# A gated linear recurrence with a feed-forward block behind it: q and k transposed by DMA from slab 8, f16 sums and an SBUF carry from the second block, one product for q and k, a new order

## The chip, the cores and the metric

The kernel runs on one core of a Trainium2 chip. A core has five engines, each with an instruction queue of its own that is worked off in order: TensorE (PE, matmuls; its weight loads are listed as PEld), VectorE (DVE), ScalarE (ACT), GpSimd (POOL) and SyncE (SP, which here issues nearly all DMA transfers). They wait for one another on semaphores. Matmul results land in PSUM, which has 8 banks of 128 x 512 f32; everything else lies in SBUF, 128 partitions wide. Transfers run on 16 DMA engines.

The metric is the device time of one execution in microseconds, median over runs.

## The reference

Sizes: batch B = 4, heads H = 8, sequence S = 768, head width D = 48, feed-forward width 1536.

```
scale = min(|a|, 0.999) / (|a| + 1e-6);   a_n = a * scale        # a = a_re + i a_im, per position and channel
for t in range(S):
    S_re, S_im = a_re_n*S_re - a_im_n*S_im + k[t] v[t]^T,  a_re_n*S_im + a_im_n*S_re
    y[t] = q[t] . S_re
x   = y as [B*S, H*D] = [3072, 384]
out = (sigmoid(x @ w_gate) * (x @ w_val)) @ w_out
```

So a linear attention whose state decays and turns by a complex factor per step, then a gated feed-forward block. The output is f32, [3072, 384].

## The kernel before, in words

**Slabs.** The sequence is cut into 6 blocks of 128 steps; a slab is one block of one batch element, 24 in all, numbered block by block (slab m is block m // 4, batch element m % 4). Slabs are handled in 8 groups (`SIZES` = 2, 2, 4, 4, 4, 4, 2, 2); groups 0 and 1 are block 0, group 2 is block 1, groups 6 and 7 are block 5.

**Running sums in place of the recurrence.** Within a block the product of the factors up to step t is exp(sum of log magnitudes) times a turn by the sum of the angles. Per slab:

- `lr`, `la` load a_re and a_im; `sq`, `add` form the squared magnitude; `lna`, `lnm`, `inv` (Ln, Ln, Exp on ACT), `lh` (the cap), `r` and `atan` (the angle), the ACT steps once per group.
- `cl` (L664, L668): a matmul with a triangular matrix gives the running sum of log magnitudes. Groups in `SPLIT` use two f16 matmuls, a high part (`lh`) and a low part (`ll`, on DVE, L637); the others use one f32 matmul, which the trace records as two instructions. `ee` takes exp of it with both signs.
- `ct` (L794): the same for the angles. Split groups first form a high part `th` and a low part `tl` (L779, DVE). `r16` and `nid` (L809, L816) take the whole turns off.
- **The carry.** The angle at the end of a block must be added in the next. `cr` (L826) copies the last rows of the sum of slab b into rows 32b to 32b+31 of a tile. For block 1 (`0 < c <= PECARRY`) a matmul with `sel_t` (L799) adds it in PSUM. For blocks 2 to 5 `car` (L749, on SP) writes the four rows of that tile to DRAM, and `hop` (L756, on POOL, an accumulating transfer) adds them to the first row of the angles, behind `atan` and ahead of `th`.
- `ab`, `cs` (Abs and two Sin on ACT, in PSUM) give cosine and sine. `ks` and `qs` (L862, both DVE) multiply k and q (scaled by `qke`) with them into a slot of two tiles; six slots go round.
- For the scores q and k must lie with channels on partitions. Slabs below 12: `tp` (L905, L906), 16 TensorE transposes into PSUM in two halves, and `qkT` (L912, DVE) copies each half to SBUF. Slabs in `CROSSED` (12 to 23): `xk` and `xq` (L883), transposing DMA transfers issued on SP.
- `sc` (L924) the scores, `mst` (L939) the causal mask, `kv` and `P` (L971, L981) the state update, `u` and `x16` the decayed state for the next block, `y` (L997, L999) the output, `y16`, `xp`, `xt` bring it, transposed, to the feed-forward block.

**Feed-forward.** Pairs of slabs (`PAIR` = 2) go through six rounds of `pg`, `pv` (L1056, 6 matmuls of 256 columns each), `tanh` (L1067, ACT) and `p` (L1074, DVE), then `po` (L1095), `ot` and the store `st`. Three `xt` and three `p` tiles allow three pairs in flight.

**What sets the order.** Every step has a due time in the table `TIMES`. The function `order` sorts all steps by due time; each engine gets its instructions in that order and never passes a waiting one. `SLOTS` says which buffer (which PSUM bank, for `ps`) each step takes, in the order of first use. `HOME` gives, for steps that several engines can do, one letter per slab (per pair for `lh`, `r`, `th`): v DVE, a ACT, g POOL. `WARM` puts matmuls of zeros ahead of some steps. ACT's function tables are reloaded (L1138) where the order asks for another set.

Of the kernel before, what the change touches and what calls it, by code (L numbers as in the profile page):

```python
# [27 lines left out]
CROSSED = range(12, 24)  # L28
YCROSSED = ()
PAIR = 2  # L30
PECARRY = 1
SPLIT = range(3, 8)
MSTP = ()
HOME = {
    "sq": "vavvgaagaggagagavaaggggg",
    "add": "gggvggvvgggggggggggggggg",
    "lh": "vggggggggggg",
    "r": "vvggvgggvggg",
    "v16": "gggaggagggggggaaagggvggv",
    "qke": "vvvggggggggggggggggggggg",  # L40
    "th": "aaaavvaaggvv",
    "ab": "vvaaaaaaavaaaavaaaaaavaa",
    "u": "gggggggggggggggvgggg",
    "x16": "ggggggggggvgggag",
    "y16": "vvaaaaaaavavvaaaaavavaaa",
    "xt": "vvaavvavvvvavavvavvvaaaa",
    "ot": "vaaavvavaavavaaaaaavavava",
# [4 lines left out]
        34.76, 27.25, 44.96],  # L52
    "wv": [
        36.69, 44.14, 47.99],
    "wo": [
        63.7, 71.27, 80.15],
    "lr": [
        0.75, 1.65, 12.17, 12.18, 15.95, 26.45, 24.02, 15.96, 37.53, 42.64,
        54.85, 37.54, 58.8, 63.25, 87.47, 78.78, 95.08, 110.69, 105.75,
        114.39, 170.85, 174.29, 130.56, 139.74],  # L60
    "la": [
        1.12, 4.55, 12.22, 12.2, 19.37, 25.84, 21.22, 16.03, 42.84, 42.83,
        53.55, 44.17, 80.31, 59.39, 76.31, 78.76, 107.5, 95.09, 117.2, 119.03,
        170.87, 174.28, 139.73, 134.75],
    "sq": [
        4.54, 6.39, 12.23, 12.21, 21.17, 27.26, 24.93, 19.27, 49.71, 42.85,
        55.51, 53.38, 81.42, 80.11, 88.29, 90.2, 115.95, 126.32, 117.31,
        127.19, 176.25, 177.54, 155.55, 165.32],
    "add": [
        6.4, 7.31, 12.44, 12.45, 23.07, 30.13, 25.79, 24.29, 52.32, 54.49,  # L70
        56.06, 56.07, 83.14, 87.29, 98.5, 94.17, 119.01, 127.85, 126.29,
        128.49, 176.26, 179.52, 155.57, 165.52],
    "lna": [
        7.32, 12.83, 30.15, 57.36, 94.15, 129.61, 180.39, 165.33],
    "lh": [
        10.88, 13.61, 30.14, 26.43, 64.31, 64.98, 101.75, 107.3, 134.76,
        140.3, 182.76, 169.83],
    "lnm": [
        12.47, 15.44, 31.38, 58.76, 101.74, 130.55, 181, 165.54],
    "inv": [  # L80
        7.9, 13.59, 31.37, 66.41, 94.18, 135.41, 180.4, 165.34],
    "r": [
        8.79, 15.45, 34.73, 34.72, 70.42, 69.22, 96.98, 101.73, 138.82, 139.7,
        180.42, 179.54],
    "cl": [
        15.49, 15.46, 19.34, 21.21, 36.7, 34.06, 31.47, 38.64, 74.99, 66.39,
        67.33, 68.54, 104.43, 105.41, 108.6, 112.42, 145.37, 136.86, 146.77,
        143.53, 184.79, 185.77, 172.31, 172.64],
    "ee": [
        15.9, 15.48, 24.01, 25.83, 38.98, 38.19, 37.4, 40.76, 75.51, 67.18,  # L90
        67.86, 69.16, 106.4, 106.51, 110.29, 112.99, 146.78, 137.85, 147.62,
        144.73, 186.41, 187.2, 174.3, 173.16],
    "scr": [
        25.85, 33.29, 31.51, 31.5, 52.27, 52.93, 51.21, 47.17, 78.8, 78.75,
        79.05, 78.79, 117.22, 114.38, 121.64, 120.31, 154.92, 148.93, 150.85,
        148.91, 193.01, 193.02, 185.81, 187.21],
    "rbt": [
        33.49, 34.96, 54.47, 80.32, 126.28, 155.54, 195.56, 198.13],
    "arr": [
        34.71, 36.72, 56.03, 81.16, 126.73, 155.99, 197.32, 199.92],  # L100
    "lk": [
        12.19, 12.46, 21.28, 29.68, 26.44, 48.23, 42.63, 55.5, 64.32, 78.77,
        68.33, 64.97, 110.67, 96.74, 95.11, 108.94, 102.79, 145.39, 138.23,
        145.62, 147.68, 165.3, 187.24, 187.22],
    "lq": [
        12.24, 13.6, 21.95, 31.49, 31.48, 51.2, 42.67, 58.78, 66.4, 83.19,
        69.2, 92.61, 112.7, 96.75, 106.52, 118.39, 105.76, 154.09, 154.91,
        147.66, 185.12, 168.96, 202.83, 187.26],
    "lv": [
        13.62, 27.35, 15.47, 33.78, 59.27, 59.25, 72.81, 65.62, 92.62, 76.82,  # L110
        98.51, 94.16, 118.36, 112.69, 118.02, 147.65, 161.33, 145.61, 165.55,
        133.7, 178, 187.25, 145.6, 208.24],
    "v16": [
        15.43, 32.35, 37.52, 36.75, 60.61, 61.26, 73.19, 66.75, 95.1, 76.83,
        110.26, 114.74, 119.98, 126.08, 125.91, 150.87, 165.56, 145.71,
        171.38, 137.86, 201.11, 188.09, 202.82, 213.05],
    "qke": [
        19.36, 16.02, 24.92, 34.87, 41.51, 52.28, 47.18, 58.79, 81.41, 84.14,
        80.33, 98.48, 118.19, 110.61, 126.3, 119.99, 148.92, 156, 158.45,
        168.57, 196.68, 192.98, 206.64, 191.8],  # L120
    "atan": [
        9.99, 19.31, 36.74, 71.94, 103.78, 140.31, 183.16, 184.81],
    "ct": [
        10.87, 12.16, 21.18, 27.27, 37.41, 45.83, 41.33, 51.19, 78.06, 81.17,
        84.17, 88.31, 112.74, 114.95, 122.26, 124.27, 147.09, 152.92, 163.2,
        166.33, 189.04, 188.71, 201.82, 200.42],
    "r16": [
        19.28, 15.91, 21.19, 28.21, 39.67, 48.9, 44.18, 52.45, 78.74, 81.4,
        84.19, 91.31, 113.27, 116.35, 122.79, 125.25, 147.61, 154.08, 165.57,
        167.78, 191.29, 189.24, 202.38, 201.83],  # L130
    "nid": [
        19.29, 15.94, 21.2, 30.12, 40.75, 50.35, 44.79, 53.37, 80.1, 84.16,
        84.23, 95.06, 114.37, 117.19, 123.9, 125.89, 148.28, 154.72, 166.17,
        168.59, 192.14, 190.02, 205.29, 204.07],
    "cr": [
        19.33, 21.23, 21.27, 34.74, 41.1, 52.3, 47.13, 53.95, 83.15, 87.38,
        86.81, 95.66, 114.73, 119.02, 127.22, 128.51, 150.86, 157.12, 167.36,
        168.95],
    "ab": [
        19.32, 19.3, 21.96, 32.37, 41.09, 52.29, 47.14, 54.84, 83.2, 86.85,  # L140
        86.82, 96.76, 117.32, 119.18, 124.29, 128.5, 152.28, 157.11, 166.97,
        169.87, 195.82, 190.82, 206.62, 205.63],
    "cs": [
        19.35, 21.24, 21.97, 34.75, 42.73, 52.33, 47.15, 56.04, 84.18, 88.32,
        86.84, 96.77, 118, 119.97, 127.23, 128.52, 152.3, 157.13, 167.76,
        170.15, 196.48, 191.79, 208.25, 205.64],
    "ks": [
        21.25, 21.94, 27.34, 37.42, 45.18, 52.92, 48.24, 59.38, 84.21, 88.36,
        87.36, 98.49, 120.32, 122.63, 127.84, 129.14, 153.43, 157.77, 169.85,
        174.96, 196.69, 193, 210.87, 206.28],  # L150
    "qs": [
        21.26, 23.09, 28.68, 37.59, 45.19, 55.52, 48.25, 60.62, 86.8, 89.74,
        88.3, 99.12, 121.63, 123.92, 128.54, 129.58, 153.44, 158.42, 170.16,
        174.97, 196.7, 193.63, 210.88, 206.65],
    "tp": [
        23.08, 25.81, 27.29, 25.8, 32.34, 29.67, 39.45, 40.77, 47.12, 47.77,
        56.59, 56.15, 51.18, 62.13, 63.23, 66.72, 88.44, 87.35, 92.59, 95.63,
        93.04, 94.14, 106.39, 100.14],
    "qkT": [
        23.68, 31.36, 30.17, 27.28, 33.16, 33.77, 40.14, 44.16, 50.38, 50.39,  # L160
        58.81, 59.26, 52.31, 64.33, 72.69, 69.17, 89.14, 88.34, 94.19, 96.97,
        99.53, 95.05, 107.82, 104.77],
    "sc": [
        27.79, 32.12, 31.15, 27.56, 37.93, 38.47, 41.08, 44.95, 53.53, 53.15,
        58.82, 61.25, 68.32, 68.87, 73.45, 71.92, 91.07, 90.84, 94.59, 98.88,
        108.15, 96.73, 111.48, 108.37, 126.06, 129.13, 132.19, 130.66, 142,
        139.81, 148.44, 148.67, 163.53, 160.38, 165.06, 165.29, 178.02,
        176.24, 180.57, 181.01, 202.37, 202.15, 198.9, 198.67, 216.75, 216.53,
        213.04, 212.16],
    "mst": [  # L170
        30.16, 32.56, 32.36, 31.16, 38.46, 39.07, 41.5, 47.19, 54.48, 54.56,
        59.29, 62.16, 69.19, 75.52, 76.84, 76.32, 95.04, 91.95, 95.64, 100.13,
        110.24, 97.62, 112.43, 109.59, 131.96, 132.01, 132.72, 132.21, 142.42,
        140.29, 150.22, 150.21, 165.07, 161.65, 166.19, 166.34, 179.53,
        180.41, 180.99, 182.09, 203.42, 202.81, 199.32, 200.04, 217.64,
        216.95, 215.36, 215.97],
    "kv": [
        25.82, 33.79, 40.87, 39.9, 64.09, 65.61, 75.31, 71.06, 100.86, 97.61,
        116.99, 124.06, 152.07, 143.86, 147.63, 167.81, 180.36, 169.82,
        177.12, 180.16],  # L180
    "P": [
        27.3, 34.95, 42.66, 40.74, 66.74, 66.42, 78.07, 73.71, 101.76, 101.07,
        120.33, 125.9, 156.46, 146.79, 150.2, 168.56, 183.82, 170.94, 177.52,
        185.8],
    "y": [
        33.28, 34.7, 42.62, 47.57, 65.81, 63.68, 75.54, 79.69, 98.47, 101.72,
# [200 lines left out]
def kernel(  # L387
# [12 lines left out]
    nc = tc.nc  # L400
# [134 lines left out]
    def add(key, emit, **kw):  # L535
        plan.add(key, emit, **kw)
        return key
# [637 lines left out]
```

## Time and profile before

| what | us |
|---|---|
| median of 11 runs | 251.26 (249.84 to 255.63) |
| the profiled execution | 250.66 |
| its span, first to last instruction | 248.9 |

| engine | busy us | share | instructions |
|---|---|---|---|
| PE | 222.6 | 89% | 2318 |
| DVE | 205.8 | 83% | 341 |
| ACT | 201.7 | 81% | 330 |
| POOL | 151.9 | 61% | 152 |

The DMA engines moved 38.63 MB, mostly in packets of 192 bytes (48 f32, one head of one step).

Busy time of PE is from the start of a matmul to its modelled end, and matmuls overlap: how fast PE really gets on is read from one start to the next. A row of the groups reads: line, engine, operation, out<-in by name, shapes, count, then busy us and mean ns of one, then the engine's idle time just before them and what ended it. A row of the waits reads: who waited for whom, total us, times, longest.

### The profile page before, as it was taken

The numbers are of one execution on the slowest core, as the hardware profiler recorded it, in microseconds if no ns is written. First come the engines' busy times: TensorE is split into PE (matmuls) and PEld (weight loads), VectorE is DVE, ScalarE is ACT, GpSimd is POOL, SyncE is SP. The second block draws the span as 40 slices with busy tenths as digits, with TensorE's granted clock in tenths as the row PEclk, the third lists the DMA queues.
The fourth block names the chain that finished last, engine by engine and source line by source line (L and its number), as shares of the span: only waits on it lengthen the run. The fifth ranks groups of instructions, "written<-read, shape, count | busy, mean of one in ns | idle before, by whom it ended". The sixth has DMA issues, their size and how long they took to land.

```text
span 248.9 us, 6100 instructions
## 1 busy us (share of the span) xinstructions
PE 222.6 (89%) x2318; PEld 172.8 (69%) x2318; DVE 205.8 (83%) x341; ACT 201.7 (81%) x330; POOL 151.9 (61%) x152
## 2 busy tenths in 40 slices
PE   0175899999989789999999999899999999999994
PEld 0132666678868457888767788677778877787883
DVE  6569998989889698999999979679986989878341
ACT  2999999979879589999989999787999992562441
POOL 5237596857998596777488663979567774500000
PEclk9999589999999999999999999999999999999999
DMA  7999899998999934687849998838798518563111
GB/s 141 213 207 205 162 191 209 195 210 169 189 173 188 192 79 88 124 179 175 171 89 212 202 201 154 205 90 177 165 209 178 106 67 175 122 126 76 65 66 63
DMA packets 158333, 38.63 MB, mean 155 GB/s; under 512 B 151248, under 2 KB 158304, under 8 KB 158304
## 3 DMA queue, kind: packets, MB, share of 16 engines
q1 hardware_dynamic: 154160, 34.68, 67.5%
q0 software_dynamic: 4144, 3.56, 9.5%
q8 instruction: 18, 0.29, 0.5%
q14 instruction: 11, 0.09, 0.1%
HBM read 30.70 MB, written 4.74 MB: 142 GB/s over the span
## 4 chain that ended last, share of the span: by engine, by line
PE 43%; ACT 7%; POOL 4%; DMA 2%; issue 2%; DVE 1%; SPq 1%; POOLq 0%
PE banks L1056 21%; PE banks L1095 14%; DMA v<-in_v_dram 2%; PE banks L924 2%; ACT L1138 2%; POOL a L653 1%; PE banks L794 1%; PE banks L1031 1%; ACT g L1067 1%; PE banks L999 1%; PE banks L668 1%; PE banks L997 1%; POOL qk L734 1%; PE banks L971 1%; POOL lh L628 1%
## 5 line engine op out<-in xcount | busy, mean ns | idle before, releaser
L1074 DVE SCALAR_TENSOR_TENSOR p<-g,banks 128x512 f16<-128x512 f16 x72 | 48.2, 682 | 13.3 <-ACT g L1067 6.8
L1067 ACT ACTIVATE g<-banks 128x512 f16<-128x512 f32 x72 | 41.6, 604 | 21.3 <-PE banks L1056 16.2
L1056 PE MATMUL banks<-xt,wv 128*128 128x256 f16 x432 | 57.1, 272 | 0.0
L1056 PE MATMUL banks<-xt,wg 128*128 128x256 f16 x432 | 56.4, 272 | 0.1
L1095 PE MATMUL banks<-wo,p 128*128 128x384 f16 (+1 forms) x300 | 55.0, 319 | 0.3 <-DVE p L1074 0.2
L1056 PEld LDWEIGHTS <-wg 128*128 128x128 f16 x432 | 41.0, 98 | 7.0 <-issue 1.3
L734 POOL TENSOR_TENSOR qk<-qk,ee 128x768 f32<-128x768 f32 x21 | 40.6, 1938 | 8.1 <-ACT ee L678 3.4
L1056 PEld LDWEIGHTS <-wv 128*128 128x128 f16 x432 | 40.7, 98 | 6.4 <-issue 0.2
L1138 ACT ACT_TABLE_LOAD x30 | 38.5, 1283 | 0.5
L1095 PEld LDWEIGHTS <-p 128*128 128x128 f16 x300 | 27.6, 98 | 13.2 <-issue 0.4
L939 DVE TENSOR_TENSOR mst<-banks,msk_t 128x512 f16<-128x512 f32 x48 | 31.9, 685 | 2.1 <-PE banks L924 1.6
L597 POOL TENSOR_TENSOR lm<-sq 128x384 f32<-128x384 f32 x21 | 21.9, 1050 | 12.1 <-DVE sq L591 7.8
L591 POOL TENSOR_TENSOR sq<-a 128x768 f32<-128x768 f32 x11 | 17.1, 1555 | 14.1 <-DMA a<-in_a_im_dram 10.7
L862 DVE TENSOR_TENSOR kst<-qk,banks 128x768 f16<-128x768 f32 x24 | 22.8, 949 | 1.9 <-issue 0.9
L862 DVE TENSOR_TENSOR qst<-qk,banks 128x768 f16<-128x768 f32 x24 | 22.7, 947 | 0.0
L794 PE MATMUL banks<-a,wt_t 128*128 128x384 f32 x16 | 8.9, 658 | 12.1 <-ACT a L741 11.3
L653 POOL TENSOR_TENSOR a<-a 128x768 f32<-128x768 f32 x8 | 14.5, 1814 | 4.4 <-ACT a L647 4.3
L912 DVE COPY qkT<-banks 128x1024 f16<-128x1024 f16 x24 | 16.2, 684 | 0.7 <-PE banks L906 0.7
L905 PE MATMUL banks<-idn_t,kst 128*128 128x128 f16 x96 | 14.1, 229 | 2.2 <-DVE state L981 1.1
L924 PEld LDWEIGHTS <-qkT 128*128 128x128 f16 x192 | 13.9, 100 | 2.6 <-issue 0.6
L906 PE MATMUL banks<-idn_t,qst 128*128 128x128 f16 x96 | 14.1, 230 | 0.6 <-DVE qst L862 0.6
L809 DVE TENSOR_SCALAR r<-banks 128x384 f16<-128x384 f32 x24 | 13.2, 551 | 1.3 <-PE banks L794 1.0
(95 smaller groups left out, 433.8 us busy)
## 6 DMA issues: line engine op xcount, KB each, us to landing
a<-in_a_re_dram SPq DMA_DIRECT2D x24, 192.0 KB
a<-in_a_im_dram SPq DMA_DIRECT2D x24, 192.0 KB
qk<-in_k_dram SPq DMA_DIRECT2D x24, 192.0 KB
qk<-in_q_dram SPq DMA_DIRECT2D x24, 192.0 KB
v<-in_v_dram SPq DMA_DIRECT2D x24, 192.0 KB
out_dram<-ot SPq DMA_DIRECT2D x23, 192.0 KB
wg<-in_moe_w_gate_dram POOLq DMA_DIRECT2D x3, 384.0 KB, 5.2
wv<-in_moe_w_val_dram POOLq DMA_DIRECT2D x3, 384.0 KB, 6.5
```

What stands on the lines that cost most here:

```text
L591: on.tensor_tensor(out=T[SQ], in0=T[A][:, :, s], in1=T[A][:, :, s], op=ALU.mult)
L597: home("add", m).tensor_tensor(out=T[LM][:, s], in0=T[SQ][:, 0], in1=T[SQ][:, 1], op=ALU.add)
L653: home("r", w).tensor_tensor(out=T[A][:, 1, i:j], in0=T[A][:, 1, i:j], in1=T[A][:, 0, i:j], op=ALU.mult)
L734: home("qke", m).tensor_tensor(out=T[QK], in0=T[QK], in1=T[EE], op=ALU.mult)
L862: nc.vector.tensor_tensor(out=T[SL][i].rearrange("p h (r x) -> p h r x", r=2)[:, :, :, 0:D], in0=heads(T[QK][:, i]).unsqueeze(2) .broadcas ...
L924: nc.tensor.matmul(sc[:, 4 * hf * both + i], kt, qt, start=True, stop=True)
L939: nc.vector.tensor_tensor(out=T[MS][:, :n_], in0=T[SC], in1=msk_t.unsqueeze(1).broadcast_to([L, n_, L]), op=ALU.mult)
L1056: nc.tensor.matmul(T[ACC][:, r], wt[:, j, f0:f0 + 128], T[XT][:, :, j], start=(j == 0), stop=(j == 2))
L1067: nc.scalar.activation(out=T[G16], in_=T[PG], func=FT.Tanh, scale=0.5)
L1074: nc.vector.scalar_tensor_tensor(out=T[PT][:, 2 * fp:2 * fp + 2], in0=T[G16], scalar=1.0, op0=ALU.add, in1=T[PV], op1=ALU.mult)
L1095: nc.tensor.matmul(T[PO][:, :wd], T[PT][:, fb, s0:s0 + L], wo16[:, fb, c0:c0 + wd], start=(fb == 0), stop=(fb == NFB - 1))
L1138: nc.scalar.preload_act_table_set(SETS[key[1]])
```

## The change

Five edits and new tables.

1. `CROSSED` starts at slab 8: slabs 8 to 11 are transposed by DMA too; 16 halves are left for TensorE in place of 24.
2. `PECARRY` 0: block 1 gets its carry by a `hop` as well, and `sel_t` and its matmul go. All hops (six in place of five) read the SBUF tile of `cr` directly; `car` and its DRAM tiles go. A hop waits for `atan` of its group and for `cr` of its own slabs.
3. `SPLIT` starts at group 2: the sums of slabs 4 to 7 are f16 pairs.
4. `ks` and `qs` become one product of 128 x 1536 elements (`qs`); the two tiles of a slot become one. `kv`, `tp`, `xk` and `xq` wait for it.
5. `qkT` and `P` get a letter in `HOME`; `qkT` is on DVE throughout, `P` of slab 0 on ACT.

`HOME`, `TIMES`, `SLOTS` and `WARM` are new throughout. In the new order slabs 22 and 23 come to their end before 20 and 21. The tables `TIMES` and `SLOTS` are left out here.

```diff
-CROSSED = range(12, 24)
+CROSSED = range(8, 24)
-PECARRY = 1
-SPLIT = range(3, 8)
+PECARRY = 0
+SPLIT = range(2, 8)
 HOME = {
-    "sq": "vavvgaagaggagagavaaggggg",
-    "add": "gggvggvvgggggggggggggggg",
-    "lh": "vggggggggggg",
-    "r": "vvggvgggvggg",
-    "v16": "gggaggagggggggaaagggvggv",
-    "qke": "vvvggggggggggggggggggggg",
-    "th": "aaaavvaaggvv",
-    "ab": "vvaaaaaaavaaaavaaaaaavaa",
-    "u": "gggggggggggggggvgggg",
-    "x16": "ggggggggggvgggag",
-    "y16": "vvaaaaaaavavvaaaaavavaaa",
-    "xt": "vvaavvavvvvavavvavvvaaaa",
-    "ot": "vaaavvavaavavaaaaaavavava",
+    "sq": "aavvgaaaaaaaaaggaaagaaag",
+    "add": "gvvvgggggggggvvggggvvgvg",
+    "lh": "ggvgggggggvg",
+    "r": "gggvvggggvgv",
+    "v16": "gggvgaggvvggggaggvggggvg",
+    "qke": "vvgggggggvggggggggggggvg",
+    "th": "aavggggagaag",
+    "ab": "vvavvaaavvvvaavvvaaaaaav",
+    "qkT": "vvvvvvvvvvvvvvvvvvvvvvvvvvvvvvvvvvvvvvvvvvvvvvvv",
+    "P": "avvv",
+    "u": "ggggggggggggvggvgggv",
+    "x16": "gggvggaggggvvaga",
+    "y16": "vvavaaaaavvaavaavvavaaaa",
+    "xt": "vvvvvvvavvvvvvavvvvvaaaa",
+    "ot": "vvvavvvvvvvavvavvaaavavaa",
 }
 WARM = {
-    ('ct', 2): 6,
-    ('sc', 1, 0): 5,
-    ('cl', 6): 1,
-    ('cl', 5): 2,
-    ('sc', 2, 0): 7,
-    ('cl', 7): 1,
-    ('pg', 1, 0): 1,
-    ('pv', 1, 0): 2,
-    ('pg', 1, 5): 1,
+    ('cl', 0): 10,
+    ('sc', 0, 0): 11,
+    ('sc', 1, 1): 1,
+    ('y', 0): 12,
+    ('sc', 2, 1): 1,
+    ('kv', 0): 2,
+    ('sc', 3, 0): 12,
+    ('pv', 0, 0): 3,
+    ('y', 2): 4,
+    ('pv', 0, 3): 2,
+    ('sc', 5, 1): 6,
 }
...
-        qs = const.tile([L, H, L], F16, name=f"qst{i}")
-        ks = const.tile([L, H, L], F16, name=f"kst{i}")
...
+        t = const.tile([L, 2, H, L], F16, name=f"slot{i}")
...
         if c > PECARRY:
-            if not lo:
-                def e(T, CRP=cr_tile[c - 1], c=c):
-                    nc.sync.dma_start(car[c - 1], T[CRP][31::32])
-
-                car_key = add(("car", g), e,
-                              after=[cr_key[m0 + s - B] for s in range(B)],
-                              use=[cr_tile[c - 1]])
-
-            def e(T, A=A, c=c, lo=lo, n=n):
+            def e(T, A=A, CRP=cr_tile[c - 1], lo=lo, n=n):
                 nc.gpsimd.dma_start(
-                    T[A][:1, 1, :n], car[c - 1][lo:lo + n].unsqueeze(0),
+                    T[A][:1, 1, :n],
+                    T[CRP][32 * lo + 31:32 * (lo + n):32],
                     accum_op=ALU.add)
 
-            key = add(("hop", g), e, after=[("atan", g), car_key], use=[A])
+            key = add(("hop", g), e,
+                      after=[("atan", g)] + [cr_key[m0 + s - B] for s in range(n)],
+                      use=[A, cr_tile[c - 1]])
...
-            for i, nm in ((1, "ks"), (0, "qs")):
-                def e(T, SL=SL, i=i, QK=f"qk_{m}", CS=CS):
-                    nc.vector.tensor_tensor(
-                        out=T[SL][i].rearrange(
-                            "p h (r x) -> p h r x", r=2)[:, :, :, 0:D],
-                        in0=heads(T[QK][:, i]).unsqueeze(2)
-                        .broadcast_to([L, H, 2, D]),
-                        in1=T[CS][:, :, :HD].rearrange("p r (h d) -> p h r d", d=D),
-                        op=ALU.mult)
...
+            def e(T, SL=SL, QK=f"qk_{m}", CS=CS):
+                nc.vector.tensor_tensor(
+                    out=T[SL].rearrange("p i h (r x) -> p r i h x",
+                                        r=2)[:, :, :, :, 0:D],
+                    in0=T[QK].rearrange("p i (h d) -> p i h d", d=D)
+                    .unsqueeze(1).broadcast_to([L, 2, 2, H, D]),
+                    in1=T[CS][:, :, :HD].rearrange("p r (h d) -> p r h d", d=D)
+                    .unsqueeze(2).broadcast_to([L, 2, 2, H, D]),
+                    op=ALU.mult)
+
+            add(("qs", m), e, after=[("cs", m), ("qke", m)], new=[SL],
+                use=[f"qk_{m}", CS])
...
-                add(("kv", m), e, after=[("ks", m), ("v16", m)], new=[KV],
+                add(("kv", m), e, after=[("qs", m), ("v16", m)], new=[KV],
                     use=[SL, V16])
```

## The prediction

> **What bounds the kernel now.** I read the stretches of the span first, then the PE timeline, then the groups of instructions and the waits. Stretches: start:end and length, then busy us of PE, PEld, DVE, ACT and POOL, the granted clock, the DMA share and GB/s.
>
> ```profile
> 10.90:33.00 22.10, 16.05 (x92) 10.15 (x92) 19.60 (x28) 21.69 (x33) 12.19 (x12) 0.85 1.02 193
> 33.00:100.00 67.00, 62.62 (x691) 48.23 (x689) 60.50 (x99) 59.15 (x100) 53.59 (x51) 1.00 0.94 171
> 100.00:140.00 40.00, 39.25 (x434) 31.34 (x433) 38.50 (x62) 38.18 (x61) 30.01 (x30) 1.00 0.77 159
> 140.00:200.00 60.00, 58.90 (x667) 47.50 (x666) 50.53 (x84) 55.09 (x92) 40.45 (x37) 1.00 0.80 166
> 200.00:231.00 31.00, 31.00 (x317) 23.75 (x316) 25.47 (x41) 15.89 (x33) 10.89 (x9) 1.00 0.52 113
> 231.00:248.90 17.90, 14.73 (x131) 11.85 (x127) 5.60 (x9) 6.04 (x12) 0.00 (x0) 1.00 0.19 67
> ```
>
> From 33 us on PE is busy 191.8 of 198 us up to 231. A busy matmul is not a matmul at full rate, so I also added up the usual distance from one start to the next, shape by shape (56 ns for a 128-column transpose, 109 for 256 columns, 162 for 384): 209.9 us of the 234.2 between the first start and the last. Of the 24 left over, 12.6 lie before 40 us, half clock (25.8 to 32.6 us) included, and 11 behind. So after the head **PE sets the pace, but DVE and ACT are close behind**: in 100 to 140 us DVE is busy 38.50 of 40 (96.3%) and ACT 38.18. Before 33 us PE is not the limit: ACT is busy 21.7 of 22.1 us, DVE 19.6, and the DMA share is 1.02. From 231 us on only the feed-forward part is left, with DVE at a third.
>
> **The change, TensorE.** The price of a step is read from starts (start, us, instruction):
>
> ```profile
> 36.98 0.91 PE L664 MATMUL banks<-lm,wl_t 128*128 128x384 f32 x2
> 37.73 0.33 PE L1031 MATMUL banks<-idn_t,y 128*128 128x128 f16 x3
> 37.90 0.86 PE L794 MATMUL banks<-a,wt_t 128*128 128x384 f32 x2
> 38.69 0.91 PE L799 MATMUL banks<-cr,sel_t 32*128 32x384 f32 x2
> 39.53 0.56 PE L1144 MATMUL banks<-zero 128*128 128x128 f16 x7
> ```
>
> and from the chain of work (start, time to the next piece), where the f16 form stands:
>
> ```profile
> 146.45 0.33 PE banks L668 x2
> ```
>
> An f32 sum `cl` holds PE from 36.98 to 37.73, 0.75 us; as two f16 matmuls it holds 0.33. Four slabs (4 to 7): 4 x 0.42 = 1.7 us less. The f32 sum `ct` holds 37.90 to 38.69, 0.79, against 0.33: 4 x 0.46 = 1.8. The carry product with `sel_t`, 38.69 to 39.53, goes: 4 x 0.84 = 3.4. The transposes of slabs 8 to 11 go: 4 x 16 x 0.056 = 3.6. Together **10.5 us** of PE, all of it work done after 33 us. Added are 64 warming matmuls in place of 26, 38 x 0.056 = 2.1 us. They precede steps of the head, where PE idles about 6 of 22 us; I take 0, bounds 0 and 2.1.
>
> **The change, DVE.**
>
> ```profile
> L1074 DVE SCALAR_TENSOR_TENSOR p<-g,banks 128x512 f16<-128x512 f16 x72 | 48.2, 682 | 13.3 <-ACT g L1067 6.8
> L862 DVE TENSOR_TENSOR kst<-qk,banks 128x768 f16<-128x768 f32 x24 | 22.8, 949 | 1.9 <-issue 0.9
> L912 DVE COPY qkT<-banks 128x1024 f16<-128x1024 f16 x24 | 16.2, 684 | 0.7 <-PE banks L906 0.7
> L597 DVE TENSOR_TENSOR lm<-sq 128x384 f32<-128x384 f32 x3 | 1.6, 550 | 0.0
> ```
>
> Off DVE: 8 copies `qkT` x 0.684 = 5.5. The two products of a slab, 949 ns each, start 0.87 apart and hold DVE 1.82 us. One of 1536 columns isn't in the trace; 384 columns more cost 0.948 - 0.548 (state update, 128x384) = 0.40, so 0.948 + 0.80 = 1.75. Gain 24 x 0.07 = 1.7; bounds 0 (the two already overlap all that can be saved) and 3.5 (a whole fixed part goes, 0.948 - 0.80 = 0.15). I take 1.7, from the nearest rows. On DVE: group 2 becomes split, with two `ll` of 1.00 and two `tl` of 1.22 us: 4.4. Counting the letters of the home table at the rows' own durations: `ab` 5 to 12 (7 x 0.56 = 3.9), `ot` 9 to 16 (3.7), `add` 3 to 8 (2.75), `xt` 14 to 18 (1.4), `v16` 2 to 5 (1.5), `u`, `x16`, `y16` two more each (2.9), `lh` and `qke` one more each (1.9); `sq` two fewer, `th` three fewer, `P` one fewer (-4.1). That is +14.1. Sum: 14.1 + 4.4 - 5.5 - 1.7 = 11.3; since instructions back to back start some 0.08 us before the last one's recorded end and 28 more come, it can be as low as 9. I take **+10 us on DVE**.
>
> **The others.** ACT gives up `ab`, `ot`, `xt`, `v16`, `y16` (11.2 us), takes eight `sq` (8 x 0.846 = 6.8), `x16`, `th` and a `P` (2.4), and by the new order reloads its table 29 times for 30 (1.28): -3.3. POOL gives up 21 us (`sq`, `add` above all) and takes 4. DMA: eight transposing transfers; those in the trace are 1024 packets of 256 B at 21.3 ns, 1.36 us of all 16 engines each, so +10.9 us. They come where the DMA share is 0.77 and nothing waits; I take 0, and if that cover is gone 10.9. SP issues them in 1.28 us each, 10.3 us, less four `car` issues of 0.56. Behind a waiting transpose on SP stand loads of `a`, `q`, `k`, `v` and stores:
>
> ```profile
> SPq L883 <- DVE qst L862: 12.3, 6, 5.7
> SPq L883 <- PE banks L1056: 8.1, 8, 1.3
> SPq L749 <- ACT banks L838: 3.4, 1, 3.4
> ```
>
> (waits of SP's queue: total us, times, longest). All its waits for L883 come to 35 us, 1.5 per transpose, so 12 us more, in a stretch (90 to 130 us) where it issues 24 of 40 us; loads run slabs ahead, so 0. Scores of a crossed slab start 4.8 us after its q product ends (130.6 to 135.4), by TensorE about 2.6; PE has feed-forward products (11.8 us per pair of slabs: 12 x 0.654 + 6 x 0.652) to put there. A rule speaks against this part: the Trainium skill, "VectorE: DVE Perf Modes", section "The three transpose paths", gives 390 ns for a 128x128 transpose on TensorE and 1309 ns on the crossbar, and advises TensorE where PSUM will do. By it 64 blocks would be an estimated 84 us of transfers, and the kernel would get slower; the trace, with eight blocks in 1.28 us of issue and 1.36 us of transfer, does not agree.
>
> **The carry.** Four hops now read SBUF, not the DRAM copy written by `car`. Nothing waits for `car` today: it is issued at 67.7, 104.5, 141.7 and 188.0 us, the hop 7 to 10 us behind, held by the arctangent (POOL's `hop` waited 5.9 us for ACT). So the shorter way is worth 0, plus SP's 3.4 us wait. But block 1 gets a hop that it did not have:
>
> ```profile
> L756 POOL DMA_DIRECT2D a<-car x5: 803/838/882, 77.7 to 202.0; - x5
> DMA to landing us min/median/max: 2.2/2.7/5.6
> ```
>
> It holds POOL, and what is queued there (`qke`, `lh`), for 0.84 us, and lands 2.2 to 5.6 us after its issue (5.6 is the one at 77 us, under a full DMA as here), then `th` 0.83 and `tl` 1.22 before `ct` of slabs 4 to 7. In the trace that `ct` follows its arctangent by 0.3 us (36.12 + 1.49 to 37.90); it will come 4.3 to 7.7 later. The cover is two pairs of feed-forward products, 23.6 us. I take 0; without cover 7.7. "DMA: Bandwidth & Descriptors" in the skill, section "Anatomy of one DMA", puts a transfer of this queue at about 2.0 us; by it the delay would be near the lower end, and the 5.6 us in the trace shows more.
>
> The order ends with slabs 20 and 21 in place of 22 and 23, so the last store is a whole slab, not the half that slab 23 has: about +0.3 us (`ot` 0.48 for 0.33, and twice the bytes). `kv` waits for the joint product, 0.87 us more; PE has other work. The rest of the new order I can't price: its bound is what PE stalls now, 11 us behind the head and about 6 in it, in either direction; I take 0.
>
> **The sum.** PE alone gives -10.5. DVE does not let all of it through. Between 4 and 231 us it is busy 197.4 of 227 us, 87%. With 10 more, 207.4, nothing is gained at a share of 91.4%; at 96.3%, the best that it holds over 40 us, the stretch takes 215.4 and the PE gain comes whole. I take the middle, 93.8%: 207.4/0.938 = 221.1, a gain of 5.9. The profiled execution, 250.66 us (span 248.9 and 1.8 around it), would become 244.8. The median of the runs shown, 251.26, lies 0.6 above, so **245.4 us**.
>
> **Rivals.** (1) **PE alone bounds**: DVE's waits, 13.3 us before `p` above all, are waits for PE and ACT and shrink with them. Then 251.26 - 10.5 = 240.8. For it: PE's share; against it: DVE's 96% with no wait to spare at 100 to 140. (2) **The gain is used up at the start**: the new hop, under a DMA share of 0.94 to 1.02, is not covered because the second pair's `xt` is late as well. 7.7 + 2.1 (warming) + 0.3 against 10.5 leaves 250.9. Against it: twelve products of pair 0 can be run any time. (3) **DVE becomes the bound**, the slower side: one queue in order, with more of its instructions standing between PE's product and the next one that needs its bank. It decides below a share of 91.4%; at the 90.3% of 33 to 100 us the stretch takes 229.7, +2.7 (253.9); at today's 87%, +11.4 (262.6). For it: DVE is the only engine that gets more work. Against it: POOL and ACT, which DVE waits for, get less. (4) **The crossbar does not pay**: late scores leave PE without products at 90 to 116 us and the 3.6 us come back as waits; 249.0 with the rest of the forecast. For it: the 4.8 us; against it: the products waiting.
>
> **Chances.** Forecast 0.47 (gain between 2 and 8), rival 1 0.16, rival 2 0.08, rival 3 0.21, rival 4 0.08. A measurement of this kernel tells about 0.5% (1.3 us) from no change. Faster by more: forecast, rival 1 and most of 4: 0.69. Within: 0.10. Slower: rival 3, 0.21. The range reaches from the whole PE gain with 1.3 us of the head's stalls on top, 239.5, to rival 3 at 90%, rounded up for the uncertainty of the 10 us: 255.
>
> **What would show it.** L905 and L906 64 times each, L912 16, L799 gone, L664 with eight records; L883 32 times, L756 six; one product of 1.75 us x24. DVE busy near 216 us, ACT near 198. PE's busy share from 33 us on no lower than now (rival 3: lower, with waits for DVE `qkT`, `mst`, `p`). `ct` of slab 4 some 4 to 8 us behind its arctangent, and PE busy in between (rival 2: idle). Wrong from the start: a joint product far from 1.75 us, a clock that drops again after 33 us, or PE idle at 90 to 116 us waiting for transfers.

## The result and the profile after

The changed kernel takes 256.29 us (median of 12 runs, 255.86 to 257.64) against 251.21 for the kernel before (47 runs): a ratio of 1.022, 95% interval 1.020 to 1.025. The ratio leaves out slow executions (7 of the 47, each over 1.5% above the fastest), so it is a little above the quotient of the two medians. The change makes the kernel **slower by 5.6 us** (4.9 to 6.2, the ratio's interval on 251.2), where 5.9 us of gain had been forecast. The profiled execution took 255.99 us, with a span of 254.3.

The engines' busy time, and the chain of work that ended last, in the page of after, and that chain in the page of before:

```profile
PE 218.7 (86%) x2284; PEld 170.3 (67%) x2284; DVE 215.8 (85%) x335; ACT 197.2 (78%) x318; POOL 136.5 (54%) x133
...
PE 36%; DVE 31%; ACT 11%; DMA 9%; issue 7%; POOL 3%; SPq 2%; DVEq 0%; POOLq 0%; ACTq 0%
```

```profile
PE 43%; ACT 7%; POOL 4%; DMA 2%; issue 2%; DVE 1%; SPq 1%; POOLq 0%
```

The busy times are those that were forecast (VectorE near 216 us, ScalarE near 198). The chain is another. In before it can be followed back only to 97 us (its shares add up to some 60% of the span), so I compare its pieces from there on: 106.7 us on TensorE and 2.6 on VectorE in before, 80.5 and 33.7 in after. The stretches of after, cut as those of before in the prediction (busy us of PE, PEld, DVE, ACT, POOL; clock; DMA share; GB/s):

```profile
10.90:33.00 22.10, 15.35 (x117) 10.15 (x116) 19.21 (x26) 20.99 (x35) 15.42 (x16) 0.92 1.07 196
33.00:100.00 67.00, 58.52 (x672) 47.60 (x670) 64.84 (x97) 55.81 (x88) 46.44 (x42) 0.97 0.94 174
100.00:140.00 40.00, 36.23 (x375) 27.25 (x374) 38.80 (x62) 35.02 (x56) 25.67 (x21) 1.00 0.89 171
140.00:200.00 60.00, 57.99 (x637) 45.91 (x636) 56.43 (x90) 52.37 (x85) 34.05 (x35) 1.00 0.97 191
200.00:231.00 31.00, 30.34 (x299) 23.13 (x298) 23.70 (x37) 19.24 (x37) 9.72 (x9) 1.00 0.52 107
```

From 33 to 140 us VectorE is busy 103.6 of 107 us (97%) and TensorE has dropped from 101.9 to 94.8. In before VectorE was busy 99.0 there (92.5%). The clock of 0.97 behind 33 us is one of the prediction's signs of being wrong: it was granted at half from 24.3 to 27.7 and again from 34.6 to 38.0 us. Before has as much of it, 6.8 us in one piece (25.8 to 32.6), so by its length it doesn't explain the loss. The groups that the change made or touched, and who waits for the joint product (waits: total us, times, longest):

```profile
L847 DVE TENSOR_TENSOR slot<-qk,banks 128x1536 f16<-128x1536 f32 x24 | 41.8, 1747 | 3.1 <-ACT banks L836 2.5
...
L1057 DVE SCALAR_TENSOR_TENSOR p<-g,banks 128x512 f16<-128x512 f16 x72 | 47.9, 681 | 12.3 <-PE banks L1039 10.4
```

```profile
PE banks L888 <- DVE slot L847: 6.0, 5, 1.8
PE banks L1039 <- DVE slot L847: 4.0, 6, 1.3
```

The joint product takes 1.747 us, as worked out. TensorE's transposes now wait for it, and even its feed-forward products, which don't read it; whether these wait for a bank or stand behind it in the order, the rows don't tell.

**Where the time went, in order of time.** I added up TensorE's usual start-to-start distances again (344 ns for an f32 matmul of 384 columns). The whole sum fell from 209.9 to 202.7 us, nearly the forecast amount (10.5 less 2.1 of warming), but the stalls rose from 24 to 37 us. What TensorE still has to do, by the same distances, shows where: at 30 us after has 192.2 us left against 201.6, a lead of 9.4; at 60 us 171.7 against 175.4; at 120 us 121.3 against 121.5; at 220 us 28.8 against 25.4. So 5.7 us of the lead go between 30 and 60 us, 3.5 up to 120, and 3.6 more up to 220.

The first loss is seen in block 1's arctangent: in the step of ScalarE that feeds it (`inv`, 1/|a|; first before, then after) and in the chain of after (start, us, what):

```profile
30.00 1.48 ACT L647 ACTIVATE a<-a 128x1536 f32<-128x1536 f32 x1
```

```profile
35.42 1.48 ACT L637 ACTIVATE a<-a 128x1536 f32<-128x1536 f32 x1
```

```profile
40.67 1.28 DVE mst L922 x2
41.95 0.87 DVE a L643
...
43.85 1.50 ACT a L731
45.35 0.30 issue
45.64 2.96 DMA a<-cr
48.62 2.19 DVE a L510
50.84 1.46 DVE a L764
```

ScalarE reaches `inv` 5.4 us later than in before, behind two squares and a reload of its table (31.0 to 33.9 us). In before the ratio that follows (`r`) ran on GpSimd at 32.2 us, both halves, and the arctangent ended at 37.6. In after its second half has the letter v, stands on VectorE behind two joint products, seven masks and four `qkT` copies, and comes at 41.9; from 29.4 to 42 us VectorE paused for 1 us in all. The arctangent ends at 45.35, 7.7 us later: 5.4 from ScalarE's place in the order, 2.3 from `r` on. Then the hop (2.96), `th` (2.19) and `tl` (1.46): `ct` of slab 4 has both its parts 7.0 us behind its arctangent, within the forecast 4.3 to 7.7. Together block 1's sums are some 11 us late: their `r16` starts at 52.8 for 41.6.

### The profile page after: what moved, and what is told of

It is laid out like the page before. It is cut to its first block, busy times and chain, and to the rows that moved or that the text cites. A ratio compares the mean times of both kernels' runs of the same rounds, so it can differ in the third digit from the quotient of the medians.

```text
span 254.3 us, 5999 instructions
## 1 busy us (share of the span) xinstructions
PE 218.7 (86%) x2284; PEld 170.3 (67%) x2284; DVE 215.8 (85%) x335; ACT 197.2 (78%) x318; POOL 136.5 (54%) x133
## 3 DMA queue, kind: packets, MB, share of 16 engines
q1 hardware_dynamic: 162576, 36.75, 72.8%
## 4 chain that ended last, share of the span: by engine, by line
PE 36%; DVE 31%; ACT 11%; DMA 9%; issue 7%; POOL 3%; SPq 2%; DVEq 0%; POOLq 0%; ACTq 0%
PE banks L1039 16%; DVE slot L847 12%; PE banks L1078 9%; DVE mst L922 4%; DVE p L1057 4%; DMA a<-in_a_im_dram 3%; DMA a<-cr 2%; DVE a L764 2%; PE banks L907 2%; ACT L1121 2%; ACT a L731 2%; DMA qkT<-slot 2%; POOL qk L724 1%; DVE qkT L517 1%; SPq L548 1%
## 5 line engine op out<-in xcount | busy, mean ns | idle before, releaser
L1039 PEld LDWEIGHTS <-wg 128*128 128x128 f16 x432 | 41.5, 98 | 10.5 <-issue 4.2
L724 POOL TENSOR_TENSOR qk<-qk,ee 128x768 f32<-128x768 f32 x20 | 39.8, 2000 | 13.9 <-DMA qk<-in_q_dram 9.5
L847 DVE TENSOR_TENSOR slot<-qk,banks 128x1536 f16<-128x1536 f32 x24 | 41.8, 1747 | 3.1 <-ACT banks L836 2.5
L1078 PEld LDWEIGHTS <-p 128*128 128x128 f16 x300 | 27.7, 97 | 16.7 <-issue 3.7
L587 POOL TENSOR_TENSOR lm<-sq 128x384 f32<-128x384 f32 x16 | 17.4, 1087 | 8.3 <-ACT sq L579 8.0
L510 POOL TENSOR_SCALAR v<-v 128x384 f16<-128x384 f32 x17 | 10.6, 622 | 12.5 <-DMA v<-in_v_dram 11.3
L579 ACT ACTIVATE sq<-a 128x768 f32<-128x768 f32 x17 | 14.1, 839 | 3.7 <-DMA a<-in_a_im_dram 3.5
L936 POOL TENSOR_TENSOR state<-state,arr 128x384 f32<-128x384 f32 x14 | 12.0, 872 | 7.8 <-DVE arr L693 7.8
L888 PE MATMUL banks<-idn_t,slot 128*128 128x128 f16 x64 | 10.5, 247 | 6.3 <-DVE slot L847 6.0
L508 ACT ACTIVATE y<-banks 128x384 f16<-128x384 f32 x15 | 7.5, 499 | 9.7 <-PE banks L982 9.6
L738 POOL DMA_DIRECT2D a<-cr x6 | 5.3, 890 | 15.5 <-ACT a L731 15.5
```

The costliest lines, as they stand in the source:

```text
L579: on.activation(out=T[SQ], in_=T[A][:, :, s], func=FT.Square)
L587: home("add", m).tensor_tensor(out=T[LM][:, s], in0=T[SQ][:, 0], in1=T[SQ][:, 1], op=ALU.add)
L724: home("qke", m).tensor_tensor(out=T[QK], in0=T[QK], in1=T[EE], op=ALU.mult)
L847: nc.vector.tensor_tensor(out=T[SL].rearrange("p i h (r x) -> p r i h x", r=2)[:, :, :, :, 0:D], in0=T[QK].rearrange("p i (h d) -> p i h d ...
L1039: nc.tensor.matmul(T[ACC][:, r], wt[:, j, f0:f0 + 128], T[XT][:, :, j], start=(j == 0), stop=(j == 2))
L1078: nc.tensor.matmul(T[PO][:, :wd], T[PT][:, fb, s0:s0 + L], wo16[:, fb, c0:c0 + wd], start=(fb == 0), stop=(fb == NFB - 1))
```

## Experiments

Each kernel was timed beside runs of before on the same chip; ratios are to before. After itself stands at 1.022; it was not timed again beside these runs, and before's median lay between 250.0 and 250.8 us over their chips, so differences under 1 us from after are not read. "After" or "before" in a name says which kernel was edited; the letters in the expectations name theories, explained where they are used: **D**, VectorE's load holds the kernel after (rival 3); **H**, the hop at the head does (rival 2); **L**, the joint product does by its length (in the first runs also by late deliveries, together with the crossbar); **W**, no single engine paces the kernel before.

| run | edit | median us | ratio, 95% interval |
|---|---|---|---|
| e1 | after, old `HOME` | 277.5 | 1.106 (1.099 to 1.113) |
| e2 | before, new `HOME` | 286.4 | 1.144 (1.136 to 1.152) |
| e3 | before, joint product, crossbar from slab 8, hops from SBUF | 266.4 | 1.063 (1.054 to 1.071) |
| e4 | after, block 1's carry on TensorE | 257.5 | 1.030 (1.025 to 1.035) |
| e5 | after, half the product | 245.1 | 0.979 (0.973 to 0.986) |
| e6 | before, half the product | 250.3 | 1.000 (0.997 to 1.003) |
| e7 | after, 10 of 12 blocks of `po` | 255.3 | 1.020 (1.014 to 1.026) |
| e8 | before, the same | 252.5 | 1.011 (1.005 to 1.017) |
| e9 | before, shorter sines | 249.4 | 0.996 (0.992 to 1.000) |
| e10 | after, the same | 255.4 | 1.020 (1.014 to 1.025) |
| e11 | after, old `ot`, `ab` | 259.6 | 1.037 (1.030 to 1.043) |
| e12 | e11, old `add`, `v16`, `u`, `x16` too | 265.1 | 1.058 (1.052 to 1.063) |
| e13 | after, two products | 258.5 | 1.032 (1.024 to 1.040) |
| e14 | after, a third of `p` as copies | 257.5 | 1.029 (1.022 to 1.035) |
| e15 | before, joint product | 252.3 | 1.006 (1.002 to 1.011) |
| e16 | before, 9 us more on VectorE | 253.6 | 1.013 (1.006 to 1.020) |
| e17 | after, `p` over 384 of 512 columns | 252.6 | 1.010 (1.006 to 1.013) |
| e18 | before, e6, e8 and e9 at once | 249.1 | 0.993 (0.989 to 0.996) |

### e1, e2, e11, e12: the letters alone

```diff
# e1: after.  e2: before, the other way round
-    "ab": "vvavvaaavvvvaavvvaaaaaav",
-    "ot": "vvvavvvvvvvavvavvaaavavaa",
+    "ab": "vvaaaaaaavaaaavaaaaaavaa",
+    "ot": "vaaavvavaavavaaaaaavavava",
...
```

> The changed kernel with the letters of the home table of before; order, buffers and all other edits as changed. DVE has some 14 us less to do (about 202 busy), ACT 2 more, POOL 21 more. Theory D (DVE is full from 50 to 200 us and sets the pace): 247 to 251 us, and DVE's share in 50 to 200 us falls to about 90%. Theory H (the loss is made in the head, where the sums of block 1 now wait for a hop and two DVE steps): 254 to 257, since that chain stays. Theory L (the joint product and the crossbar deliver late): 255 to 258.

> The kernel before with the new letters of the home table wherever it has the step, nothing else. DVE gets some 14 us more (about 220 busy), PE's work stays. D: 255 to 260 us. H and L: within 1.3 us of before, 250 to 252.5, because none of the steps that they blame is touched.

The first is 26 us and the second 36 us off before. Each of the exchanged kernels is far slower than both with the letters that their order was made for, although e1 has 11 us less on VectorE than after. So the two can't be told apart by exchanging all letters, and I took back smaller sets.

> The changed kernel with the letters of before for ot and ab alone: 14 operations go from DVE to ACT (DVE 7.6 us less, ACT 6.7 more, both complete, order as changed). D, at the slope that leaving out 19 us showed (11.2 us of time for 19.2 of DVE): 251 to 254 us. Against it: the order was laid out for the new homes, and ACT is full in places; then 255 to 260.

> The same, and add, v16, u and x16 with the letters of before too: 13 more operations leave DVE, most of them for POOL (DVE about 13.5 us less than after the change, 202; POOL about 7 more). D: 248 to 252 us. If POOL's slower operations (1.05 for 0.55 us) stand in the chain to the sums: 254 to 262.

Moving 14 instructions (`ot`, `ab`) from VectorE to ScalarE took 6.2 us off VectorE's busy time and cost 3.4 us; with GpSimd's letters too the loss was 9 us. A lighter VectorE did not help while the order had been made for other letters, and neither run tells how large D's share is.

### e3: crossbar and joint product put into the order of before

```diff
-CROSSED = range(12, 24)
+CROSSED = range(8, 24)
...
-                    add((nm, m), e, after=[("qs" if nm == "xq" else "ks", m)],
+                    add((nm, m), e, after=[("qs", m)],
```

The hops read SBUF here, `car` is gone, and the buffers were dealt out anew for the order of before.

> The kernel before, its order and homes, with three of the edits: the joint product (at the place of the k product), slabs 8 to 11 through the crossbar, hops out of SBUF without the DRAM copy. Block 1 keeps its carry on TensorE and its f32 sums. PE 3.6 us less, DVE 7.2 less (about 198.6). D: 247 to 249.5 us. H: no change to 1 us faster, 250 to 251.5. L: 252.5 to 256.

By TensorE's work left it is 2.2 us ahead of before at 100 us, 7.6 behind at 120 and 14.3 behind at 220. The first loss is a wait passed on: up to 94.1 us SP waits with a transposing transfer for a joint product and issues six of them up to 103.5; a store whose data were written by 96 us is queued behind them and issued at 104.9; VectorE waits for that store to give back its buffer, from 100.7 to 108.3, and TensorE for VectorE. The waits of this kernel, SP's from 86 to 106 us and then VectorE's from 100 to 125:

```profile
SPq L868 <- DVE slot L848: 9.3, 1, 9.3
```

```profile
DVE ot L511 <- DMA out_dram<-ot: 7.6, 1, 7.6
```

TensorE hardly waits for the transposing transfers themselves (0.2 us from 95 to 125), but SP's queue in order can pass a wait on. In after, where the order was made with them, SP waits 16.6 us for the joint product (longest 6.0), and one wait for a store shows, of 1.3 us. So this part of e3's loss is that of a bad place in the order; the loss behind 120 us I did not trace.

### e4: block 1's carry back on TensorE

```diff
-PECARRY = 0
+PECARRY = 1
...
```

> The changed kernel with block 1's carry back on TensorE (the f32 product with the selector, four times), so without its hop; blocks 2 to 5 hop as changed, all due times as changed. PE has 3.4 us more, DVE the same 215.8. H: the sums of slab 4 come 3 to 5 us sooner and the kernel takes 250.5 to 253.5. D: 255 to 258, since DVE stays full. L: 256 to 258.

At 257.5 it is no faster than after. Its `r16` of slabs 4 to 7 started at 54.1 to 69.6 us, no sooner than after's 52.8 to 66.2: the arctangent ended at 47.3, behind the same masks on VectorE. **H in its narrow form falls**: taking the hop away brings nothing back. But as the sums came no sooner, e4 doesn't tell what their lateness costs.

### e5, e6: less on VectorE, on the attention chain

```diff
# after; before has the same with two instructions
-                    out=T[SL].rearrange("p i h (r x) -> p r i h x",
-                                        r=2)[:, :, :, :, 0:D],
+                    out=T[SL][:, :, :, 0:D],
...
```

The product with the sines is left out; VectorE is busy 15.7 us less in e5 and 18.5 less in e6. The output is not the reference's.

> The changed kernel with half of the joint product left out: only the cosine half is multiplied, the sine half of every slot stays zero (24 products of 768 in place of 1536 elements, some 19 us less on DVE, about 196.6 busy); order, buffers, homes and every other instruction stay. Theory D (DVE is the bound after the change): 244 to 250 us. Theories H (late sums of block 1), L (late deliveries by the joint product and the crossbar) and S (SP's queue is held by waiting transposes and delivers loads late): 253 to 256.5.

> The kernel before with the same half left out of both products (48 products of 384 in place of 768 elements, some 19 us less on DVE, about 186.6 busy), nothing else changed. If PE sets the pace before the change, as the prediction had it: 249 to 251.5 us. If DVE did already then: 240 to 246.

After gains 11 us (1.022 to 0.979), before nothing: what holds the one kernel doesn't hold the other. The clock has a small part in it: two of e5's four executions, the profiled one among them, kept a mean clock of 0.998 or more (after: 0.984). The two at 0.986 took 245.5 and 246.0 us, so about 10 us remain.

### e7, e8, e9, e10: less on TensorE or ScalarE

```diff
# e7, e8
-                            for fb in range(4 * i, 4 * i + 4):
+                            for fb in ((4, 7) if i == 1 else range(4 * i, 4 * i + 4)):
# e9, e10, this line and the one for the cosine
-                nc.scalar.activation(out=T[CS][:, 1, :HD], in_=T[CS][:, 1, :HD],
+                nc.scalar.activation(out=T[CS][:, 1, :96], in_=T[CS][:, 1, :96],
```

e7 and e8 leave out 2 of 12 blocks of the last product, 7.9 us of TensorE; e9 and e10 three quarters of the sines and cosines, 10 to 11 us of ScalarE.

> The changed kernel with two of the twelve blocks left out of every sum of the last product (50 matmuls of 384 columns, 7.9 us less on PE), all else as changed. D: 254 to 256.5 us, PE's time is no longer what counts. If PE still sets the pace: 247.5 to 249.5.

> The kernel before with the same two blocks left out of the last product (7.9 us less on PE). If PE sets the pace: 242.5 to 245 us. If DVE or ACT do: 248.5 to 251.

> The kernel before with both sines taken over 96 of 384 columns (48 ACT instructions some 0.24 us shorter, 11.5 us less on ACT; the other columns stay angles). Neither 19 us of DVE nor 7.9 us of PE were worth anything before the change. Theory A (ACT paces the kernel before, its 92% of 10 to 200 us is what fills it): 240 to 246 us. Theory W (no engine alone does; the fixed order on five queues holds the time, and each engine waits in turn): 249 to 251.5.

> The changed kernel with the same 11.5 us left out on ACT. D (DVE is the bound after the change): 254 to 257 us. If ACT still paces: 246 to 250.

This is the step on which the prediction stood, tried by itself. In before 7.9 us less on TensorE give no gain at all (it is even 2.8 us slower, 1.4 to 4.2): its sum of start-to-start distances went to 202.1 us and its stalls from 24 to 33. ScalarE's 10 us are worth at most 2. In after neither is worth more than some 2 us.

### e13, e15: the joint product alone

```diff
# e15; e13 the other way round
-            for i, nm in ((1, "ks"), (0, "qs")):
...
+            add(("qs", m), e, after=[("cs", m), ("qke", m)], new=[SL],
```

> The changed kernel with the k and q products as two instructions again (k first, at the joint product's place; kv and the crossbar transfer of k wait for k alone), everything else as changed. DVE has 1.7 us more. Theory L (the length of the joint product, on which everything waits, is what costs): 251 to 254 us. Theory D (DVE's load binds): 256 to 258.

> The kernel before with the joint product in the place of the k product, and nothing else. DVE has 1.7 us less. L: 252.5 to 256 us. D, and the prediction: 249.5 to 251.5.

In after the joint product is worth about 2.5 us (0.6 to 4.5 by e13's interval). **L falls** there: the longer instruction isn't what slows after. In before it costs 1.6 us (0.4 to 2.8) although VectorE is 3.2 us less busy, between the two expectations.

### e14, e17, e16: VectorE's load off the attention chain

```diff
# e14
+                    if fp % 3 == 2:
+                        nc.vector.tensor_copy(
+                            out=T[PT][:, 2 * fp:2 * fp + 2], in_=T[G16])
+                        return
# e17
-                        out=T[PT][:, 2 * fp:2 * fp + 2], in0=T[G16],
+                        out=T[PT][:, 2 * fp:2 * fp + 2, :192],
...
...
# e16: in before, into a tile of 240 columns that nobody reads
+                    if fp % 2:
+                        nc.vector.memset(load, 0.0)
```

e14 replaces 24 of the 72 gating products by copies of the gate.

> The changed kernel with every third gating product left out (24 of the 72 p steps copy the gate, f16 in SBUF, in place of multiplying it with the value in PSUM; some 10.5 us less on DVE, none of it in the attention chain). D, at 0.58 us of time per us of DVE as in the run with half a product: 249 to 252 us. L: 254.5 to 257.

It was a weak test: the copy takes 515 ns where I had counted on some 245, so VectorE went down by 4.3 us only. But it brought no gain at all. At the 0.3 us per microsecond that e17 shows below, the ratio would have been 1.017, outside e14's interval; this stays open.

> The kernel before with 36 fills of 128x240 f32 on DVE behind every second gating product, about 10 us more on DVE (some 216 busy, as after the change), all else as before. D: 253 to 258 us. L: 250 to 252.

VectorE's busy time rose from 205.8 to 214.8 us, and the time by 3.3 us (1.5 to 5.0): nine tenths of the change's extra load, put where nothing depends on it, cost more than half of its loss (a quarter to nine tenths by the interval).

> The kernel after, with each of the 72 gating steps p over 384 of its 512 columns (the output products of the second slab of a pair read 64 columns further left, so the gated values of 64 steps are left out and the output is another). That takes some 72 x 0.13 = 9.6 us from VectorE in the feed-forward part, twice as much as the copies of the run before, and nothing from the attention chain. Theory D (VectorE's load sets the pace after the change, wherever it lies): the 0.58 us per us of the half product would give 250 to 252. Theory C (only the attention chain's own VectorE work counts, since the rows of p wait for TensorE anyway): 255 to 257.5.

VectorE went from 215.8 to 205.3 us, and the time by 3.1 us, from 1.022 to 1.010. Between the two expectations: a microsecond of VectorE's load off the attention chain is worth 0.3 us in after, as much as it cost in before (3.3 for 9.0), while on the chain (e5) it was worth 0.7 (11 for 15.7 of busy time). The same 150 us, 50 to 200, of after, of e17, of e5, of before and of e14 (columns as in the stretches above):

```profile
50.00:200.00 150.00, 137.67 (x1494) 107.58 (x1493) 144.58 (x221) 129.69 (x211) 98.04 (x91) 1.00 0.92 178
```

```profile
50.00:200.00 150.00, 140.24 (x1542) 109.89 (x1540) 140.28 (x227) 133.32 (x217) 99.11 (x92) 1.00 0.91 178
```

```profile
50.00:200.00 150.00, 144.49 (x1587) 114.26 (x1585) 138.50 (x236) 136.59 (x221) 100.14 (x93) 1.00 0.94 185
```

```profile
50.00:200.00 150.00, 144.01 (x1619) 115.83 (x1617) 133.58 (x216) 136.11 (x221) 110.06 (x105) 1.00 0.82 163
```

```profile
50.00:200.00 150.00, 136.18 (x1475) 106.33 (x1474) 141.49 (x219) 129.04 (x209) 97.82 (x90) 1.00 0.92 174
```

As VectorE goes from 144.6 to 140.3 and 138.5 us, TensorE goes from 137.7 to 140.2 and 144.5, and ScalarE with it: in these two runs only VectorE got less to do, so both had been held by it. The last row, of e14, does not follow: VectorE 141.5, TensorE 136.2.

### e18: less on three engines at once, in before

The edits of e6, e8 and e9 together, leaving out what they leave out.

> The kernel before with the three reductions that were each worth nothing, all at once: only the cosine half of both products (19 us of VectorE), 2 of 12 blocks of the last product left out (7.9 us of TensorE), the sines over 96 of 384 columns (11.5 us of ScalarE). Theory W (the engines hold one another up in turn, so that a gain shows only where all of them get less): 238 to 245. Theory O (the order's own chain of waits, loads and transfers included, holds the time whatever the engines do): 248 to 251.

At 249.1 it gains 1.9 us (0.9 to 2.9), though TensorE has 7.9 us less to do and ScalarE and VectorE are busy 10.2 and 16.6 less: W in this form falls, and the result is the one expected of **the order's own chain (O)**. O is what is left rather than shown: GpSimd (155.8 us busy) and the transfers had nothing taken away. TensorE's work left was 7.2 us less than before's at 180 us and 4.2 less at 200. Of these, 3.6 and 3.2 are products still to come that this kernel leaves out (11 and 10 slabs x 2 x 0.162), so a real lead of 3.6 us shrank to 1.0 in 20 us, where the chain of this kernel runs over queued issues of SP and a load of `q`:

```profile
188.71 1.65 SPq L559
190.35 0.04 issue
190.40 0.58 SPq L559
190.98 0.04 issue
191.03 3.04 DMA qk<-in_q_dram
```

## Why the prediction was wrong, step by step

- **"So after the head PE sets the pace, but DVE and ACT are close behind."** This is the step that failed. TensorE was busy 191.8 of 198 us, and yet 7.9 us taken from it are worth nothing (e8). In before an engine relieved only waited longer for the next: TensorE's stalls rose by 9 us when 7.9 us of its work went (e8), and VectorE's 18.5 us (e6) were worth nothing either. The 10.5 us were worked out nearly right (7.2 net of about 2 for warming, 8.4 forecast) and sold at the wrong price. One reservation: e8 takes work from the feed-forward part, the change from the sums and transposes; that part of the work could not be taken away from before alone without its new order.
- **"I take the middle, 93.8%".** The second step that failed. VectorE's load was right (215.8 us for 215.8; that it is right to the tenth is luck, as the working gave 9 to 11.3 more). But from 4 us to the last `y16` (236.3) it is busy 208.4 of 232.3 us: a share of 89.7%, below the 91.4% at which nothing is gained and next to the 90.3% of rival 3, whose 253.9 is the nearest of all the figures. 97% is held from 33 to 140 us only; from 10.9 to 33 it is 87%, and from 200 to 231 76%. The middle between 91.4 and 96.3% had no row behind it. So **rival 3 came true**: VectorE's load holds after (e5, e17; e14 doesn't show it), and the load alone costs time in before (e16). Its sign came too: from 33 to 231 us TensorE is busy 183.1 of 198 us (191.8 in before), though its waits for VectorE are mostly for the joint product, not for `qkT`, `mst` or `p`.
- **What VectorE costs.** 10 us at the 0.36 us that e16 shows per microsecond is 3.6 of the 5.6 lost (1.7 to 5.5 by e16's interval). The other 2 us are not settled; the late start of block 1 is the place that the trace offers for them.
- **"The carry, cover 23.6 us, I take 0."** The delay behind the arctangent was right (7.0), and taking the hop away brings nothing (e4). What the prediction left unpriced ("the rest of the new order I can't price") is larger: the arctangent itself comes 7.7 us later, 5.4 of it because ScalarE reaches `inv` later and 2.3 because a letter moves half of `r` behind VectorE's masks. That reading is from the trace; neither was put back by itself, so what it costs isn't shown.
- **Joint product: 1.75 us forecast, 1.747 measured.** Gain in load right (1.4 to 3.2 us in e13 and e15), worth about 2.5 us in after; in before the joint product costs 1.6 (e15).
- **The crossbar**: the packets' time in the main queue went up by 17 us of all engines (67.5% of 248.9 to 72.8% of 254.3) for the 10.9 forecast, and the DMA share from 140 to 200 us from 0.80 to 0.97. TensorE hardly waits for transfers in after, but GpSimd does, nearly all of it behind 140 us (waits: total us, times, longest):

```profile
POOL v L510 <- DMA v<-in_v_dram: 11.3, 4, 7.6
POOL qk L724 <- DMA qk<-in_q_dram: 9.5, 1, 9.5
```

In before these two come to 0.5 and 3.3 us. So the cover on which the prediction took 0 was thinner than it said. Late loads and rival 4 were not tried in after itself; e5 speaks against their being the limit, as it gains 11 us with GpSimd's same two waits at 21.7 us. In e3 the loss that I traced came from SP's order.
- **The tail, +0.3**: from the end of the last `p` to the end 6.6 us for 5.4, so +1.2.

Whether a version with the change's smaller TensorE work and before's VectorE load would beat both stays open; each set of letters taken back (e1, e11, e12) would need an order of its own, and none was made. No complete kernel tried here is faster than before.

## What to carry to other kernels

A busy share of 97% doesn't say that an engine sets the pace: take some of its work away and look, before selling a gain on it. In this kernel, with a fixed order on several queues, work removed from one engine of before was worth nothing to 2 us, and work added to VectorE off the chain cost about a third of its length (e16). In after, where VectorE is nearly full for 100 us, work removed from it was worth 0.3 of its length off the chain (e17, not seen in e14) and 0.7 on it (e5). Letters, order and buffers are one design: exchanging letters alone cost 3 to 36 us here.

## What was not expected of the hardware

An f16 copy of 128 x 512 from SBUF to SBUF took 515 ns on VectorE (e14), 1.0 ns a column, only a quarter less than the gating product of the same size with a PSUM operand (681 ns). The accumulating transfer from SBUF took 3.2 and 2.6 us from issue to landing (medians for 6 and 3 KB), the one from DRAM 4.4 and 2.3, with five or six transfers in all and the DMA engines loaded differently; a shorter landing by the way over SBUF isn't shown. In e3 the granted clock fell to 0.69 between 105 and 120 us, where TensorE was busy 11.1 of 15 us; before kept 1.00 there with 14.9 busy. So a stretch of half clock (104.0 to 114.2 us) lay over TensorE's stall and the work behind it; that the stall brought it about isn't shown.
